# Attention in the order of a build-time list scheduler, with a third of p transposed on TensorE and q, k split before they are transposed

## The chip, the cores and the metric

The kernel runs on one core of one Trainium2 chip. The metric is the device time of one execution in microseconds; 773.15 us is the median of three runs of the kernel before (771.51 to 775.70).

## What is computed

An attention of 2 x 8 heads over 768 rows of 64 elements, masked by equality of 6-bit hash buckets, then two mixing layers on the joined heads (512 wide):

```python
q_bits = (einsum('bhsd,dk->bhsk', q, proj) > 0); k_bits = (einsum('bhsd,dk->bhsk', k, proj) > 0)
mask = bucket(q_bits)[..., :, None] == bucket(k_bits)[..., None, :]
scores = where(mask, q @ k.T / sqrt(64), -1e9)
x = softmax(scores) @ v                       # heads side by side: (2, 768, 512)
x_prev = x shifted down by one row
xk, xr = mu_k * x + (1 - mu_k) * x_prev, mu_r * x + (1 - mu_r) * x_prev
y = sigmoid(xr @ w_r) * (relu(xk @ w_k) ** 2 @ w_v)
u = y + (y.T @ U @ V).T
out = u + relu(u @ w_ch1) @ w_ch2
```

The weights come as 64-bit floats.

## The kernel before

Numbers that need more than the short format of TensorE are kept as a high and a low part, and products are made of several matmuls of parts. One core does it all, in program order on each engine.

**Attention.** Each of the 16 heads has 6 tiles of 128 rows, 96 tiles in all. Per head, q and k are loaded in natural layout (`nq`, `nk`), transposed on TensorE by threes (`prep_T`, L302) into the PSUM tile `pt`, and split there: ScalarE writes the rounded high part into one half of the partitions of `yq`, `yk` (`prep_h`, L314), VectorE the rest into the other half (`prep_l`, L319). A DMA moves the high part to a second tile `xq`, `xk` (`prep_x`, L327), `prep_z` (L334) makes the hash products, `prep_bits` (L340) their signs, and two DMAs bring these as mask rows behind x (`prep_mask`, L347). GpSimd splits v into parts (`prep_v`).

Per tile: `scores` (L369, L370; four matmuls into `ps`, one of three double banks of PSUM), `row_max` (L374), two small steps (L378, L382), `exps` on ScalarE (L388, writes `p`), `part1` (p rounded to 16 bits; L395 on ScalarE for four tiles of six, L393 on VectorE for two), `part2` on GpSimd (the rest; L124), `transp` (L404: one DMA transpose of both parts, issued from SyncE, into one of six tiles `pT`) and `weighted` (L418: 30 matmuls against v). At the end of a head come sums and division (L426 to L439); of each pair of heads `to_xT_pe` (L449) and L452 make the transposed input of the mixing layers.

**Order.** A hand-made table holds one entry for each step with an offset in tiles; for each tile number n the loop goes through it and issues the step of tile n minus offset. So `("tile", -1, "scores")` and `("tile", 6, "av")` put the product of a tile seven tiles behind its scores. `DRAIN` holds pieces of the first mixing layer (`shift_a`, `shift_b`: x mixed with the row ahead and split; `r`: nine matmuls each, eight of them) for the last tiles. `TICKS` says at which tiles the weight conversion goes one step on.

**Weights.** A job loads 64-bit words (`conv_load`, L155, three buffers `raw`), makes single precision of them on ScalarE (L167, L168), VectorE (L172, L176) and GpSimd, and splits (`conv_split`). A pipeline tick does one stage of each of the jobs under way.

**Queues.** SyncE issues the transposes, the masks of q and the weights; ScalarE issues the loads of q, k and v, the moves of y and the masks of k, between its computing.

**Behind attention** the mixing layers follow in code written out in its order: `k_half` and `halves` run k, `k_act` and v of one layer after the other, in PSUM tiles that attention leaves free. The second batch's and the channel layers are of the same kind.

## Time and profile before

| | us |
|---|---|
| median of three runs | 773.15 |
| span of the profiled execution | 780.9 |
| first exp of a tile begins | 19.23 |
| last exp ends | 306.5 |
| first matmul of the first layer's k stage | 329.2 |

| engine | busy us | share | instructions |
|---|---|---|---|
| TensorE | 700.5 | 90% | 5792 |
| VectorE | 500.2 | 64% | 866 |
| ScalarE | 390.1 | 50% | 630 |
| GpSimd | 331.4 | 42% | 252 |

The page gives the profiled execution's span, from the first to the last instruction, and no other time of it. Busy shares are means over two unlike halves; the tables of stretches separate them. [...]

### The profile page before, as it was taken

To read this page: it belongs to the slowest core of one execution; us is meant where nothing else is said; L and a number is where in the kernel's file an instruction comes from. 1 tells how busy PE (TensorE), PEld (TensorE's weight loads), DVE (VectorE), ACT (ScalarE), POOL (GpSimd) and SP (SyncE) were. 2 spreads that over 40 slices of the span, in tenths; PEclk is the share of its full clock that TensorE was granted. 3 is DMA by queue.
4 is the path that set the end of the run, shared out by engine and by line. 5 is a ranking of instruction groups with operands and counts; after the bars stand their busy time and mean duration, and the time that the engine had idled before them with its cause. 6 is when DMAs were issued, how large, how long until landed. Compare 5 with 4: busy or idle time off the path is not lost.

```text
span 780.9 us, 14599 instructions
## 1 busy us (share of the span) xinstructions
PE 700.5 (90%) x5792; PEld 614.3 (79%) x5792; DVE 500.2 (64%) x866; ACT 390.1 (50%) x630; POOL 331.4 (42%) x252
## 2 busy tenths in 40 slices
PE   4879778767798888989999999999999999999997
PEld 3668677766687776878878888888899989999996
DVE  5879997857788779589977998612578432111112
ACT  4767677655667675586546865421445221111110
POOL 1677677655676775366734754230333100000000
PEclk9889999878799999999999999999999999999999
DMA  6899999999999998123101333100334010000002
GB/s 210 140 239 210 222 207 204 220 161 167 193 206 224 182 199 128 42 87 129 48 27 55 109 109 107 54 15 14 93 124 134 1 45 37 1 1 1 0 1 81
DMA packets 180291, 86.41 MB, mean 111 GB/s; under 512 B 154432, under 2 KB 172992, under 8 KB 180224
## 3 DMA queue, kind: packets, MB, share of 16 engines
q1 hardware_dynamic: 170512, 69.36, 45.1%
q10 hardware_dynamic: 9712, 16.13, 9.4%
q8 instruction: 45, 0.74, 0.4%
q14 instruction: 22, 0.18, 0.1%
HBM read 37.10 MB, written 3.15 MB: 52 GB/s over the span
## 4 chain that ended last, share of the span: by engine, by line
PE 57%; DVE 21%; DMA 11%; issue 5%; ACT 3%; POOL 2%; SPq 1%; ACTq 1%; DVEq 0%; POOLq 0%
PE ps L605 9%; PE ps L607 8%; PE ps L606 8%; PE pt L607 7%; PE pt L605 7%; PE pt L606 7%; DMA pT<-p 7%; DVE nm L374 4%; PE pt L418 3%; DVE w L124 3%; DVE raw L172 2%; DMA xq<-zt 2%; PE ps L334 2%; ACT p L388 2%; DVE p L393 1%
## 5 line engine op out<-in xcount | busy, mean ns | idle before, releaser
L124 POOL TENSOR_TENSOR p<-p,p 128x768 f16<-128x768 f32 x96 | 159.5, 1667 | 75.3 <-ACT p L395 24.4
L676 DVE SCALAR_TENSOR_TENSOR hl<-pt,hl 128x384 fp32r<-128x384 f32 x64 | 35.7, 557 | 173.1 <-ACT hl L675 173.1
L418 PEld LDWEIGHTS <-pT 128*128 128x128 f16 x2880 | 104.4, 102 | 39.1 <-issue 31.9
L418 PE MATMUL pt<-v,pT 128*128 128x64 bf16 (+1 forms) x2880 | 115.3, 200 | 21.0 <-DVE xn L439 16.3
L675 ACT ACTIVATE hl<-pt 128x384 fp32r<-128x384 f32 x64 | 31.4, 491 | 200.2 <-PE pt L607 200.2
L124 POOL TENSOR_TENSOR cx<-cx,raw 128x512 int32<-128x512 int32 (+2 forms) x55 | 79.7, 1450 | 99.5 <-DVE cx L176 62.7
L388 ACT ACTIVATE p<-ps,nm 128x768 f32<-128x768 f32 x96 | 94.8, 989 | 54.0 <-DVE nm L382 29.5
L607 PE MATMUL ps<-w,hl 128*128 128x512 f32 x288 | 113.8, 395 | 3.5 <-DVE hl L594 3.4
L605 PE MATMUL ps<-w,hl 128*128 128x512 f32 x288 | 114.7, 398 | 2.0 <-ACT y L575 1.5
L606 PE MATMUL ps<-w,hl 128*128 128x512 f32 x288 | 113.1, 393 | 0.0
L374 DVE TENSOR_REDUCE nm<-ps 128x1 f32<-128x768 f32 x96 | 91.5, 953 | 16.3 <-PE ps L370 14.8
L369 PE MATMUL ps<-xk,xq 76*128 76x384 f32 x192 | 78.8, 411 | 14.9 <-ACT p L388 7.1
L605 PE MATMUL pt<-ut,w 128*128 128x384 f32 x256 | 86.5, 338 | 0.0
L607 PE MATMUL pt<-ut,w 128*128 128x384 f32 x256 | 86.1, 337 | 0.0
L124 DVE TENSOR_TENSOR w<-cx,w 128x512 fp32r<-128x512 f32 (+2 forms) x55 | 77.8, 1415 | 13.0 <-ACT w L208 13.0
L606 PE MATMUL pt<-ut,w 128*128 128x384 f32 x256 | 85.9, 336 | 0.0
L370 PE MATMUL ps<-yk,yq 128*128 128x384 f32 x192 | 70.4, 367 | 0.0
L607 PEld LDWEIGHTS ps<-w,hl 128*128 128x128 f32 x288 | 54.0, 188 | 19.3 <-DVE hl L594 7.9
L605 PEld LDWEIGHTS ps<-w,hl 128*128 128x128 f32 x288 | 54.1, 188 | 14.6 <-ACT y L575 2.2
L606 PEld LDWEIGHTS ps<-w,hl 128*128 128x128 f32 x288 | 54.1, 188 | 8.5
L395 ACT ACTIVATE p<-p 128x768 f16<-128x768 f32 x64 | 54.0, 844 | 9.6 <-DMA pT<-p 5.2
L369 PEld LDWEIGHTS ps<-xk,xq 76*128 76x128 f32 x192 | 40.6, 211 | 18.8 <-ACT p L388 9.9
(123 smaller groups left out, 1290.8 us busy)
## 6 DMA issues: line engine op xcount, KB each, us to landing
raw<-in_moe_w_ch_dram SPq DMA_DIRECT2D x32, 512.0 KB
raw<-in_moe_w_k_dram SPq DMA_DIRECT2D x8, 512.0 KB
raw<-in_moe_w_v_dram SPq DMA_DIRECT2D x8, 512.0 KB
nk<-in_k_dram ACTq DMA_DIRECT2D x16, 192.0 KB
xq<-yq ACTq DMA_DIRECT2D x16, 192.0 KB
xk<-yk ACTq DMA_DIRECT2D x16, 192.0 KB
v<-in_v_dram ACTq DMA_DIRECT2D x16, 192.0 KB
nq<-in_q_dram ACTq DMA_DIRECT2D x15, 192.0 KB
```

Source lines behind the costliest of these rows:

```text
L124: eng.tensor_tensor(out=out, in0=a, in1=b, op=op)
L369: nc.tensor.matmul(s_ps[:, j, 0:G], d["xq"][:, qc], d["xk"][:, c], start=True, stop=False)
L370: nc.tensor.matmul(s_ps[:, j, 0:G], d["yq"][:, qc], d["yk"][:, c], start=False, stop=True)
L374: nc.vector.tensor_reduce(out=nm[:, 0:1], in_=tl[n]["s"][:, :, 0:G], axis=AX.XY, op=ALU.max, negate=True)
L388: nc.scalar.activation(p, tl[n].pop("s")[:, :, 0:G], AF.Exp, bias=nm[:, 2:3], scale=nm[:, 1:2])
L395: nc.scalar.activation(p12[:, 0], tl[n]["p"], AF.Copy)
L418: nc.tensor.matmul(o[:, 0:d], pT[:, part, kt, :], V[a][:, kt, 0:d], start=(kt == 0 and (part, a) == (0, 1)), stop=(kt == NT - 1 and (part, ...
L605: nc.tensor.matmul(o, sh, mh, start=first, stop=False)
L606: nc.tensor.matmul(o, sh, ml, start=False, stop=False)
L607: nc.tensor.matmul(o, sl, mh, start=False, stop=last)
L675: nc.scalar.activation(hl[:, 0], self.o, AF.Relu)
L676: nc.vector.scalar_tensor_tensor(out=hl[:, 1], in0=self.o, scalar=0.0, in1=f(hl)[:, 0], op0=ALU.max, op1=ALU.subtract)
```

## The change

The order of attention is no longer a table. `Plan` collects every step as an operation with the engines that may do it and a cost for each, what it comes after, a due number and the buffers that it takes and frees; `order` goes through time and gives each free engine the ready operation with the smallest due number. Where two engines may do a step, the free one with the smaller cost gets it. The program is then issued in that order, so each engine's order is fixed when the kernel is built.

Steps that change: (1) q and k are split in natural layout, high part by ScalarE or VectorE (`prep_H`), low part by GpSimd (`prep_L`); high and low lie side by side, so two groups of three transposes (`prep_T`) give half of y each, which ScalarE copies out whole (`prep_E`); hash products and bits go by halves through the `pt` tile. (2) Tiles 1 and 4 of a head are transposed on TensorE in single precision (`flip`, six transposes into a `ps` tile), then rounded by ScalarE and subtracted by VectorE out of PSUM, with no DMA. (3) `part1` of the other tiles goes to ScalarE or GpSimd. (4) All DMAs are issued from SyncE. (5) Eight weight jobs run in attention, and the shifts of the first mixing layer are planned one by one; its eight r products come after the last tile's product and division.

```diff
+PE_TILES = (1, 4)
+JOBS_EARLY = 8
+SLOTS = {"s": 3, "t": 1, "o": 1, "n": 4, "hl_q": 1, "hl_k": 1, "y_q": 2, "y_k": 2, "x_q": 2, "x_k": 2, "zt": 2,
+         "p": 3, "p12": 4, "pT": 6, "xn": 2, "raw": 3, "cx": 4, "xh": 8, "sq": 3, "v": 2, "nm": 4}
...
+            ready.sort(key=lambda op: op.due)
+            for op in ready:
+                on = [e for e in op.on if clock[e] <= now]
+                if not on or any(free_slots[s.kind] < 1 for s in op.take):
+                    continue
+                e = min(on, key=lambda x: op.on[x])
...
+                if e == "sp":
+                    clock[e] = now + 0.1
+                    wire = max(wire, now + 1.3) + cost
+                    op.end = wire + 0.8
+                else:
+                    op.end = clock[e] = now + cost
...
+    def prep_H(i, s, e):
+        t = hd[i]["hl" + s] = ap.tile([128, NT, 2, D], F32R, name=f"hl_{s}", bufs=1)
+        copy(e, t[:, :, PART[s]], hd[i]["n" + s])
+
+    def prep_L(i, s, e):
+        t = hd[i]["hl" + s]
+        minus(e, t[:, :, 1 - PART[s]], hd[i].pop("n" + s), f(t)[:, :, PART[s]])
...
+    def flip(n):
+        f_ps = tl[n]["f"] = psum_s()
+        p = tl[n].pop("p")
+        for j in range(NG):
+            for i in range(TG):
+                c = slice(i * 128, (i + 1) * 128)
+                nc.tensor.transpose(f_ps[:, j, c], p[:, j, c], ident)
...
+        nc.scalar.activation(p1, src, AF.Copy)
...
+        minus("dve", flipped(n, 1)[0], src, p1)
...
-    def prep_h(i, s):
-    def prep_l(i, s, e):
...
+            sc = add({"pe": 0.74}, lambda e, n=n: scores(n), [*masks, *xs, *y_done], n - 1.5, take=[s_s],
+                     free=[*toks["q"], *toks["k"]], lag=0.25)
...
+            if t in PE_TILES:
+                f_s = Slot("s")
+                fl = add({"pe": 0.5}, lambda e, n=n: flip(n), [ex], n - 0.5, take=[f_s], free=[p_s], lag=0.25)
+                p1 = add({"act": 0.86}, lambda e, n=n: flip_part1(n), [fl], n - 0.5, take=[pT_s])
+                got = add({"dve": 0.98}, lambda e, n=n: flip_part2(n), [p1], n - 0.5, free=[f_s])
+            else:
+                c_s = Slot("p12")
+                p1 = add({"act": 0.87, "pool": 1.0}, lambda e, n=n: part1(n, e), [ex], n + 0.5, take=[c_s])
+                p2 = add({"pool": 1.7}, lambda e, n=n: part2(n), [p1], n + 0.5, free=[p_s])
+                got = add({"sp": 2.4}, lambda e, n=n: transp(n), [p2], n, take=[pT_s], free=[c_s])
+            avs.append(add({"pe": 0.97}, lambda e, n=n: weighted(n), [got, v2], n + 3, take=[] if avs else [o_s],
+                           free=[pT_s, v_s], lag=0.25))
...
+            r_last = add({"pe": 2.1}, lambda e, g=g, c=c: mixes[0].r(g, c), [lows[-1], r_last, sig, *tail], N + 30 + j, free=[h_s],
+                         lag=0.25)
```

On SyncE at the start of the program stood, before (`xq<-zt` is the mask of the first q; that of k was on ScalarE's queue):

```order
L239 DMA nq<-in_q_dram 128x384
L248 DMA p_raw<-in_proj_dram 64x6 x2
L459 DMA mu_k<-in_moe_mu_k_dram 128x4x1
L459 DMA mu_r<-in_moe_mu_r_dram 128x4x1
L155 DMA raw<-in_moe_w_r_dram 128x1024 x3
L347 DMA xq<-zt 12x768
```

Now, from the 14th row on, with 12 transfers of the first heads and weights ahead (three of them `raw`):

```order
L288 DMA nq<-in_q_dram 128x384
L379 DMA xk<-yk 64x768
L288 DMA nk<-in_k_dram 128x384
L379 DMA xq<-yq 64x768
L192 DMA raw<-in_moe_w_r_dram 128x1024
L288 DMA nq<-in_q_dram 128x384
L192 DMA raw<-in_moe_w_k_dram 128x4x256
L396 DMA xk<-zt 12x768
L396 DMA xq<-zt 12x768
```

The first masks stand behind the loads of two or three heads and behind five weight loads, where three stood ahead of them.

In the middle of attention stood on SyncE, before:

```order
L404 DMA_TRANSPOSE pT<-p_2308 128x12x128
L404 DMA_TRANSPOSE pT<-p_2419 128x12x128
L347 DMA xq<-zt 12x768
L404 DMA_TRANSPOSE pT<-p_2434 128x12x128
L404 DMA_TRANSPOSE pT<-p_2487 128x12x128
L404 DMA_TRANSPOSE pT<-p_2585 128x12x128
L404 DMA_TRANSPOSE pT<-p_2593 128x12x128
L404 DMA_TRANSPOSE pT<-p_2642 128x12x128
L404 DMA_TRANSPOSE pT<-p_2747 128x12x128
L347 DMA xq<-zt 12x768
L404 DMA_TRANSPOSE pT<-p_2763 128x12x128
L404 DMA_TRANSPOSE pT<-p_2816 128x12x128
```

and now, over about as many tiles:

```order
L452 DMA_TRANSPOSE pT<-p_2169 128x12x128
L452 DMA_TRANSPOSE pT<-p_2242 128x12x128
L288 DMA nk<-in_k_dram 128x384
L379 DMA xk<-yk 64x768
L379 DMA xq<-yq 64x768
L452 DMA_TRANSPOSE pT<-p_2351 128x12x128
L452 DMA_TRANSPOSE pT<-p_2363 128x12x128
L396 DMA xk<-zt 12x768
L396 DMA xq<-zt 12x768
L288 DMA nq<-in_q_dram 128x384
L452 DMA_TRANSPOSE pT<-p_2473 128x12x128
L288 DMA v_1_125<-in_v_dram 128x384
```

Six transposes of a head have become four, and the loads of q, k and v (L288), the moves of y (L379) and both masks (L396) stand between them.

On VectorE in the middle of attention stood, before (L319 is the low part of y, L393 the rounded p, L340 the hash bits; names carry their buffer numbers):

```order
L382 TENSOR_SCALAR nm_2534<-nm_2534 128x1
L393 CAST p12_2585<-p_2536 128x768
L374 TENSOR_REDUCE nm_2587<-ps_2542 128x1
L378 TENSOR_SCALAR nm_2587<-nm_2587 128x1
L319 TENSOR_TENSOR yq_2578<-pt_2538,yq_2578 64x3x128
L382 TENSOR_SCALAR nm_2587<-nm_2587 128x1
L374 TENSOR_REDUCE nm_2638<-ps_2597 128x1
L319 TENSOR_TENSOR yq_2578<-pt_2538,yq_2578 64x3x128
L378 TENSOR_SCALAR nm_2638<-nm_2638 128x1
L382 TENSOR_SCALAR nm_2638<-nm_2638 128x1
L374 TENSOR_REDUCE nm_2697<-ps_2645 128x1
L378 TENSOR_SCALAR nm_2697<-nm_2697 128x1
```

and now (L161 with `pT<-ps` is the subtraction for a tile transposed on TensorE, L349 the high part of k, L423, L427 and L431 the row maximum and the two small steps):

```order
L423 TENSOR_REDUCE nm_2941<-ps_2884 128x1
L427 TENSOR_SCALAR nm_2941<-nm_2941 128x1
L431 TENSOR_SCALAR nm_2941<-nm_2941 128x1
L161 TENSOR_TENSOR pT_2992<-ps_2950,pT_2992 128x768
L349 CAST hl_k_3009<-nk_2353 128x6x64
L423 TENSOR_REDUCE nm_3016<-ps_3002 128x1
L423 TENSOR_REDUCE nm_3032<-ps_3011 128x1
L427 TENSOR_SCALAR nm_3016<-nm_3016 128x1
L427 TENSOR_SCALAR nm_3032<-nm_3032 128x1
L431 TENSOR_SCALAR nm_3016<-nm_3016 128x1
L431 TENSOR_SCALAR nm_3032<-nm_3032 128x1
L423 TENSOR_REDUCE nm_3083<-ps_3026 128x1
```

The low parts of y and the casts of p are gone from between the row maxima, and the subtraction out of PSUM and the copies of q and k have come in; two row maxima now also stand together ahead of their small steps.

## Rows read from the trace of the kernel before

**Rows 1.** the page, parts 1 and 2: span, and DMA share in 40 equal slices.

```profile
span 780.9 us, 14599 instructions
...
DMA  6899999999999998123101333100334010000002
```

**Rows 2.** stretches; columns: us, busy PE, PEld, DVE, ACT, POOL (instructions), PEclk, DMA share, GB/s.

```profile
19.20:306.50 287.30, 230.11 (x3329) 203.23 (x3328) 233.65 (x468) 192.82 (x253) 193.22 (x136) 0.88 1.15 196
...
54.00:72.00 18.00, 16.38 (x261) 14.93 (x262) 15.77 (x33) 12.71 (x17) 13.99 (x10) 0.91 1.20 216
...
162.00:180.00 18.00, 11.90 (x147) 10.22 (x147) 10.02 (x21) 9.73 (x14) 9.69 (x7) 0.72 1.22 190
...
252.00:270.00 18.00, 14.50 (x242) 12.83 (x238) 15.12 (x33) 13.62 (x17) 13.91 (x10) 0.98 1.16 193
```

**Rows 3.** the same view of line L388 alone, the exps.

```profile
252.00:270.00 18.00, 7.56 (x8) 0.98 1.16 193
```

**Rows 4.** SyncE's queue in time (start us, us, instruction, count), then line L404's durations in ns.

```profile
93.86 16.30 SPq L404 DMA_TRANSPOSE pT<-p  x6
...
280.84 20.25 SPq L404 DMA_TRANSPOSE pT<-p  x9
...
L404 SPq DMA_TRANSPOSE pT<-p x96: 1274/2388/5505, 24.1 to 309.9; - x96
```

**Rows 5.** durations (ns, min/median/max) of other transfers' issue, by line.

```profile
L347 SPq DMA_DIRECT2D xq<-zt x16: 756/784/1553, 13.2 to 279.9; - x16
...
L327 ACTq DMA_DIRECT2D xq<-yq x16: 496/500/543, 7.9 to 265.4; - x16
...
L239 ACTq DMA_DIRECT2D v<-in_v_dram x16: 330/334/580, 19.3 to 285.4; - x16
```

**Rows 6.** the chain that ended last, in order of time: start us, us, what.

```profile
13.21 3.14 DMA xk<-zt
...
112.11 8.21 DMA pT<-p
...
130.42 4.72 DMA pT<-p
...
311.54 0.23 PE ps L606
...
319.77 0.95 PE pt L418 x30
```

**Rows 7.** VectorE by line from 19.2 to 306.5 us; the fourth: the whole run.

```profile
L374 DVE TENSOR_REDUCE nm<-ps 128x1 f32<-128x768 f32 x95 | 90.5, 953 | 16.2 <-PE ps L370 14.8
...
L393 DVE CAST p<-p 128x768 f16<-128x768 f32 x31 | 23.6, 761 | 20.2 <-ACT p L388 17.3 <-DMA pT<-p 1.9 <-ACT yq L314 0.7
...
L319 DVE TENSOR_TENSOR yk<-pt,yk 64x384 fp32r<-64x384 f32 x28 | 15.6, 556 | 0.9
...
L124 DVE TENSOR_TENSOR ut<-pt,ut 128x384 fp32r<-128x384 f32 x16 | 8.8, 552 | 10.4 <-ACT ut L208 10.4
```

**Rows 8.** ScalarE by line from 19.2 to 306.5 us.

```profile
L395 ACT ACTIVATE p<-p 128x768 f16<-128x768 f32 x64 | 54.0, 844 | 9.6 <-DMA pT<-p 5.2 <-issue 2.3 <-PE ps L370 0.2
```

**Rows 9.** GpSimd by line from 19.2 to 306.5 us.

```profile
L124 POOL TENSOR_TENSOR p<-p,p 128x768 f16<-128x768 f32 x95 | 157.8, 1667 | 74.8 <-ACT p L395 24.4 <-DVE p L393 18.2 <-DVE rl L426 17.1
...
L124 POOL TENSOR_TENSOR v<-v 128x384 f32<-128x384 f32 x32 | 27.9, 871 | 22.6 <-DMA v<-in_v_dram 20.6 <-ACT p L388 1.7 <-ACT yk L314 0.2
```

**Rows 10.** instructions in order of time: start us, us, engine, line, instruction.

```profile
60.52 0.52 PE L302 MATMUL pt<-ident,nq 128*128 128x128 f32 x3
...
60.80 0.42 PE L369 MATMUL ps<-xk,xq 76*128 76x384 f32 x1
...
19.23 0.99 ACT L388 ACTIVATE p<-ps,nm 128x768 f32<-128x768 f32 x1 [1.44 <-DVE nm L382]
...
306.52 1.65 DVE L393 CAST p<-p 128x768 f16<-128x768 f32 x1 [0.28 <-ACT p L388]
...
329.22 0.42 PE L605 MATMUL pt<-xh,w 128*128 128x384 f32 x1
```

382 lines of the change are left out of this document (229 added, 153 removed).

## The prediction

> **What bounds the kernel now.** I read the page first: the sixteen DMA engines are full in the slices up to about 300 us and nearly empty behind [rows 1]. So the run has two halves. Until 329.2 us it is attention; there the first matmul of the first mixing layer's k stage starts [rows 10]. From there to the end, 451.7 us, TensorE is busy almost without a gap and the code is the same in both kernels. What the change is worth is decided ahead of 329.2 us.
>
> I split that half at the exps, one for each of the 96 tiles. Start: 19.2 us to the first exp. Middle: 287.3 us from the first to the last, 2.99 us a tile. Drain: 22.7 us from the last exp's end at 306.5 us to 329.2 us [rows 2, 10].
>
> In the middle no computing engine is full: TensorE 230 us, VectorE 234, ScalarE 193, GpSimd 193 of 287.3, while the DMA share stands at 1.15 [rows 2]. The queue that carries it is SyncE's. Six transposes of p occupy it for 16.3 us, 2.72 us each, their median is 2.39 us, and nine with hardly a load beside them take 20.25 us, 2.25 us each [rows 4]. 96 x 2.72, 16 masks of 0.78 us and 8 weight loads, taken like the moves of y at 0.50 us [rows 4, 5], make 278 us of 287.3: the queue is the bound. The chain of waits agrees, with pieces of 8 us at a transpose [rows 6]. Where the queue lets go, eight tiles pass in 18 us [rows 3].
>
> **The change part by part.**
>
> *DMA and SyncE.* 32 of 96 transposes leave the queue, and all other transfers of attention move from ScalarE's queue into it. By issue time: 64 x 2.25 to 2.72 = 144 to 174 us, 32 masks x 0.78 = 25, 32 moves of y x 0.50 = 16, 48 loads x 0.33 = 16, 12 weight loads x 0.5 = 6 [rows 4, 5]. Together 207 to 237 us, some 10 of them ahead of the first exp, so 197 to 227 us instead of 278. It stops being the bound. A transpose that waits here for GpSimd's subtraction now holds back every load and mask behind it; the second rival prices that.
>
> *ScalarE.* It loses the issue of 47 loads (0.33), 32 moves (0.50) and 16 masks (0.79), 44 us on top of its 193 us [rows 5]. Of the rounded copies of p it keeps 23, and gains 32 of transposed tiles: nine fewer x 0.84 us [rows 8]. Splits of q and k and more shifting work put about 12 us on. Some 197 us: not the bound.
>
> *VectorE*, in the middle, from 234 us. Removed: 31 casts of p, 23.6 us, and the low parts of y, 56 x 0.555 = 31.1 us [rows 7]. Added: 32 subtractions for the transposed tiles. Before has none of this shape with its input in PSUM; the nearest are 128x384 with one input in PSUM in 0.552 us, twice that is 1.10, and the row maximum, which reads as many elements from PSUM in 0.953 us [rows 7]. I take 1.0, 32 us. Of the 32 high parts of q and k it gets 20, about 17 of them in the middle; half a cast of p is 0.38 us on the mean [rows 7], I take 0.45, 7.6 us. Copies of xT 3, weight words 5 less (more jobs are done ahead of the first exp), shifting of the first mix 4 more. 234 - 54.7 + 32 + 7.6 + 3 - 5 + 4 = 220 us; 216 to 244 between the bounds, the upper end if each high part takes the 1.65 us of the slowest cast [rows 10] (at the share taken below that is 782 us).
>
> *GpSimd*, from 193 us: 32 subtractions of p at 1.667 us fewer, -53.3; 28 low parts of q and k, like the 128x384 subtractions for v at 0.871 us [rows 9] or a little dearer, +26; other moves +2. Then 41 rounded copies of p, which the trace doesn't show on this engine. They read one operand instead of two, so from half the subtraction, 0.83 us, to all of it, 1.667. I take 1.0: 168 + 41 = 209 us, 202 to 236 between the bounds.
>
> *TensorE.* Three transposes take 0.28 us from start to start [rows 10]. Six for each of 32 tiles, 18 us, and for q and k 28 triples more in the middle, 8 us. From 230 us at a mean clock of 0.88 [rows 2], 202 at the full clock, to 228; this counts the ends of bursts, so it is an upper value. The busier stretch of 252 to 270 us had 0.98 [rows 2]; there 228 is 233 us.
>
> *So the middle* has VectorE at 220 busy us with a small pause after each of its 480 or so instructions, TensorE and GpSimd close behind. What share can VectorE reach? In two stretches where the queue hardly stopped it: 15.77 of 18 us from 54 us on, 88%, and 15.12 of 18, 84%, in the fastest [rows 2, 3]. I take 85%, since four other engines are now nearly as full: 220 / 0.85 = 259 us, 2.70 us a tile.
>
> *Start.* The masks, on which the first scores wait, are issued at 13.2 us and land 3.1 us later [rows 6]. In the new order of SyncE the second weight load ahead of them needs a raw buffer, and so the second integer addition on GpSimd. Ahead of this on GpSimd stand four low parts, four steps for v, an addition and a weight subtraction: with itself eleven operations of 0.87 us or a third more [rows 9], about 11 us with pauses. They begin when the first k is loaded and rounded, at some 8 us (an estimate; before, the whole preparation takes until 13.2). So the masks go out at 19.5 us. Two masks of 0.78, 3.1 us to land, then scores, row maximum and the two small steps: first exp at 25.5 us, 6.3 later. Lower bound none (if GpSimd is quicker than that), upper bound 10.
>
> *Drain.* After the last exp: the rounded copy 0.84 to 1.65, the subtraction 1.67, a transpose of 4.72 us when the queue is free, its product 0.95, the sums and the division about one row maximum, 1.0, three transposes 0.3, and all eight r products, which the planner holds until the attention is done: 72 matmuls x 0.23 us = 16.5 us [rows 6 to 10]. About 26.4 us for 22.7, where half of the r work lay between the last tiles. Shifts of the k part run on VectorE, ScalarE and GpSimd under those 16.5 us, two for each 4 us; without that cover they would cost 1 us each.
>
> *Behind it* one weight job more is ready; TensorE idles only some us there, so I book nothing.
>
> Sum: 25.5 + 259 + 26.4 = 310.9 for 329.2 us, -18.3 us. The profiled execution has a span of 780.9 us [rows 1] and the median of the runs is 773.15, 0.99 of it, so -18.1: **755 us**.
>
> **The rivals.** (a) *Better packing.* The list scheduler lets VectorE reach 94%: 220 / 0.94 = 234 us, -43 us, 730 us. For it: several engines are at or below 230 us. Against it: no stretch of 18 us shows it with eight tiles.
>
> (b) *The transposes' way becomes the bound; slower.* Before, the product of a tile stands on TensorE seven tiles behind its scores; now four to six, five on the mean by the order. From scores to product lie 0.7 + 0.95 + 0.4 + 0.99 + 0.84 + 1.67 = 5.6 us of work (the first and third estimated) and the transfer [rows 7 to 10]. At 4.72 us that is 10.3 us, and 2.7 us a tile leaves 14.6. At 8.21 us, as under load [rows 6], it is 13.8, with 2 to 3 us of queueing at three engines 16.5; over 5.4 tiles 3.05 us a tile, a middle of 293 us, +15.5 us, 789 us. It decides at 2.89 us a tile (277 us), once a transfer takes over about 7.5 us. For it: one queue for everything, in order. Against: a quarter of its time is free now.
>
> (c) *GpSimd's copies cost the full 1.667 us*: 236 / 0.85 = 278 us, +1 us, 774 us.
>
> (d) *TensorE at a low clock.* In 162 to 180 us its clock was 0.72 with the engine waiting for transfers [rows 2]. If new waits hold it at 0.80, 228 / 0.80 = 285 us, +7.6 us, 781 us. The Trainium skill's page TensorE: Matmul & The Clock Gate, section on PE-mode transpose, says that a transpose doesn't count as a busy TensorE for the clock; by that rule the added 26 us of transposes would favour this case. No run here shows it yet: the transposes of before are too few.
>
> (e) *Transposes were not the limit.* Then VectorE keeps the 81% that it has over the whole middle [rows 2]: 220 / 0.81 = 272 us, -5 us, 768 us. The Trainium skill's page Advanced Engine Details and Errata, section X-Bar Transpose (TRN2), says that a transposing transfer is as fast as a plain one, which speaks for this and against the change. The trace is against it: 393 KB in 2.25 us, 175 GB/s, below the 196 GB/s of the mixed middle, and the queue's own 278 us [rows 2, 4].
>
> **How the numbers follow.** Forecast (VectorE between 82 and 90%: 740 to 764 us) 50%, (a) 13%, (b) 15%, (c) 10%, (d) 7%, (e) 5%. A difference of 0.5%, 4 us, is about what a measurement of this kernel can tell from no change. Faster by more than that: the forecast and (a) wholly, a fifth of (c), over half of (e): 68%. Within it: half of (c), parts of (b), (d) and (e): 11%. Slower: the rest of (b), (c) and (d), 21%. The range from 733 to 785 leaves out half of (a) and the upper part of (b), together under 20%.
>
> **What would show it.** Right: 64 transposes on SyncE, the first exp near 25.5 us, the last ending near 284, the first k matmul near 311, and about 452 us behind it; VectorE at 85% in the middle with 1.0 us for the new subtraction; GpSimd's copies at 1.0 us. (b) shows as TensorE's products waiting for transposed p for many us in all, (c) as GpSimd over 90% busy, (d) as a mean clock under 0.85, (a) as a middle under 245 us. The forecast is wrong above all if buffers or waits, not one full engine, set the pace.

## The result, and the profile after

The changed kernel takes 785.44 us (median of four runs, 782.72 to 786.28), the kernel before 772.68 us (median of four runs): 1.0147 times as long, 95% interval 1.0108 to 1.0186. The prediction was 755 us, in a range of 733 to 785 us, and faster; the kernel became 1.5% slower.

The page of the changed kernel, parts 1 and 2, against [rows 1]: the span is the same 780.9 us, and the DMA engines, full before up to 300 us, have room.

```profile
span 780.9 us, 15090 instructions
...
PEclk9988999999999999999999999999999999999999
DMA  7599688797878767033201333100333010000002
```

Two equal spans and two unequal times: a run's time is its span and mostly 1.8 us, so the changed kernel's profiled execution (782.7 us) is one of its ordinary runs, while that of the kernel before, some 782.7 us by the same sum, is 10 us longer than the median of its ordinary runs. The experiments come back to this.

The stretch from the first to the last exp, then two parts of it (columns as in [rows 2]). TensorE is the fullest engine, and from 100 us on at its full clock.

```profile
32.60:302.30 269.70, 237.51 (x3637) 215.22 (x3636) 213.98 (x446) 181.69 (x263) 204.20 (x169) 0.97 0.81 153
...
40.00:100.00 60.00, 51.15 (x718) 46.99 (x717) 49.47 (x90) 38.32 (x56) 45.60 (x36) 0.89 0.86 167
100.00:280.00 180.00, 164.17 (x2584) 149.28 (x2583) 141.56 (x308) 123.92 (x183) 139.61 (x119) 1.00 0.83 155
```

Instructions in time at the start, answering [rows 10] (19.23 us for the first exp): the load of the first k; on TensorE the first transposes of the second head; on SyncE a weight load and the first mask behind it; on TensorE hash products of the second head and only then the scores of tile 0; the first two exps.

```profile
3.19 0.50 SPq L288 DMA_DIRECT2D nk<-in_k_dram  x1
...
18.55 0.87 PE L368 MATMUL pt<-ident,hl_k 128*128 128x128 f32 x3 [0.87 <-DVE zt L390]
...
21.34 0.38 SPq L192 DMA_DIRECT2D raw<-in_moe_w_k_dram  x1
...
21.77 0.89 SPq L396 DMA_DIRECT2D xk<-zt  x1
...
24.51 0.65 PE L385 MATMUL pt<-yk,wb_both_k 128*108 128x384 f32 x1 [0.58 <-ACT yq L347]
...
28.32 0.52 PE L418 MATMUL ps<-xk,xq 76*128 76x384 f32 x1
...
32.60 1.87 ACT L437 ACTIVATE p<-ps,nm 128x768 f32<-128x768 f32 x2 [1.51 <-DVE nm L431]
```

And at the end of attention, where the kernel before has its first k matmul at 329.22 us: the product of the last tile, the first r product behind it, and the first matmul of the k stage.

```profile
309.25 1.83 PE L488 MATMUL pt<-v,pT 128*128 128x65 bf16 x30 [2.84 <-DMA pT<-p]
...
312.71 0.78 PE L687 MATMUL ps<-w,xh 128*128 128x512 f32 x1
...
331.01 0.33 PE L687 MATMUL pt<-xh,w 128*128 128x384 f32 x1
```

By these the profiled executions split so:

| us | before | forecast | after |
|---|---|---|---|
| start, to the first exp | 19.2 | 25.5 | 32.6 |
| middle, first to last exp | 287.3 | 259 | 269.7 |
| drain, to the first k matmul | 22.7 | 26.4 | 28.7 |
| behind it | 451.7 | 451.7 | 449.9 |
| span and 1.8 | 782.7 | 764.4 | 782.7 |

### The profile page after: what moved, and what is told of

It reads as the page before. It is cut to its first block, busy times and chain, and to the rows that moved or that the text cites. A ratio compares the mean times of both kernels' runs of the same rounds, so it can differ in the third digit from the quotient of the medians.

```text
span 780.9 us, 15090 instructions
## 1 busy us (share of the span) xinstructions
PE 718.8 (92%) x6080; PEld 634.8 (81%) x6080; DVE 475.3 (61%) x830; ACT 377.8 (48%) x633; POOL 356.9 (46%) x301
## 4 chain that ended last, share of the span: by engine, by line
PE 65%; DVE 14%; DMA 6%; POOL 4%; issue 4%; ACT 4%; SPq 1%; DVEq 0%; ACTq 0%; POOLq 0%
PE ps L687 9%; PE ps L689 9%; PE ps L688 9%; PE pt L689 7%; PE pt L687 7%; PE pt L688 7%; PE pt L488 5%; DMA pT<-p 3%; DVE nm L423 2%; DVE w L161 2%; PE ps L418 2%; PE pt L368 2%; PE pt L385 2%; DVE raw L209 2%; PE ps L419 2%
## 5 line engine op out<-in xcount | busy, mean ns | idle before, releaser
L161 POOL TENSOR_TENSOR cx<-cx,raw 128x512 int32<-128x512 int32 (+2 forms) x55 | 79.8, 1451 | 89.9 <-DVE cx L213 55.5
L488 PE MATMUL pt<-v,pT 128*128 128x64 bf16 (+1 forms) x2880 | 106.8, 195 | 10.6 <-DMA pT<-p 8.0
L488 PEld LDWEIGHTS <-pT 128*128 128x128 f16 x2880 | 99.7, 98 | 20.0 <-DMA pT<-p 10.3
L161 POOL TENSOR_TENSOR p<-p,p 128x768 f16<-128x768 f32 x64 | 107.9, 1693 | 11.8 <-ACT p L347 10.5
L437 ACT ACTIVATE p<-ps,nm 128x768 f32<-128x768 f32 x96 | 92.6, 989 | 34.3 <-DVE nm L431 25.6
L423 DVE TENSOR_REDUCE nm<-ps 128x1 f32<-128x768 f32 x96 | 90.3, 951 | 21.3 <-PE ps L419 20.5
L418 PE MATMUL ps<-xk,xq 76*128 76x384 f32 x192 | 73.8, 384 | 9.9 <-ACT p L437 4.2
L161 DVE TENSOR_TENSOR w<-cx,w 128x512 fp32r<-128x512 f32 (+2 forms) x51 | 72.5, 1424 | 5.0 <-ACT w L253 3.5
L419 PE MATMUL ps<-yk,yq 128*128 128x384 f32 x192 | 67.3, 351 | 0.0
L687 PEld LDWEIGHTS ps<-w,hl 128*128 128x128 f32 x288 | 54.1, 188 | 14.2 <-ACT y L657 1.7
L349 POOL CAST p<-p 128x768 f16<-128x768 f32 x41 | 35.5, 867 | 35.1 <-ACT p L437 34.9
L687 PEld LDWEIGHTS pt<-ut,w 128*128 128x128 f32 x256 | 48.1, 188 | 2.4
```

The source lines that it names most:

```text
L161: eng.tensor_tensor(out=out, in0=a, in1=b, op=op)
L349: (nc.vector if e == "dve" else nc.gpsimd).tensor_copy(dst, src)
L418: nc.tensor.matmul(s_ps[:, j, 0:G], d["xq"][:, qc], d["xk"][:, c], start=True, stop=False)
L419: nc.tensor.matmul(s_ps[:, j, 0:G], d["yq"][:, qc], d["yk"][:, c], start=False, stop=True)
L423: nc.vector.tensor_reduce(out=nm[:, 0:1], in_=tl[n]["s"][:, :, 0:G], axis=AX.XY, op=ALU.max, negate=True)
L437: nc.scalar.activation(p, tl[n].pop("s")[:, :, 0:G], AF.Exp, bias=nm[:, 2:3], scale=nm[:, 1:2])
```

## The experiments

All tables below give the first exp, the middle and the drain of the profiled execution, and the run time: the median where the kernel was timed, else its single profiled run. "Before" was 771 to 775 us in each of these sittings.

### The kernel before once more, and without its transposition

> The kernel before, unchanged, profiled once more. The profiled execution that the prediction was worked out on has a span of 780.9 us, though its runs are 771.5 to 775.7 us, and one stretch of it (160 to 216 us) had eleven us or so more than its neighbours: 15 exps in 56 us at a granted clock of 0.78. Theory A: that execution was a long one; an ordinary one has the first exp at 19 us, the first matmul of the k stage near 320 us instead of 329.2, so a middle of about 278 us (2.89 us a tile), and 452 us behind it. Then the two kernels differ by 12 us in the middle of an ordinary execution, not by the 17.6 us that the two profiles show. Rival B: the middle of 287 us is ordinary, and the profiler makes the difference: a span of 780 us again, with the k stage at 329 us.

The profiled execution took 787.2 us, the eleven ordinary ones of the same sitting 768.5 to 780.3, median 773.7. So B of that text holds: the long middle comes with the profile. The second experiment replaces the transposing transfer of p by a plain one of the same bytes.

```diff
-        nc.sync.dma_start_transpose(
-            out=pT.rearrange("p a b c -> p (a b) c"), in_=tl[n].pop("p12").rearrange("p a g c -> p (a g c)")
+        nc.sync.dma_start(
+            out=pT.rearrange("p a b c -> p (a b c)"), in_=tl[n].pop("p12").rearrange("p a g c -> p (a g c)")
```

> The kernel before, but the transfers of p on SyncE's queue copy the same 393 KB without transposing them; the transposition is left out. Theory A (the prediction's view): the transposes of 2.25 to 2.72 us in SyncE's queue are the bound of the attention before; copied plainly the queue has room, and the middle falls from 287 to 290 us (in a profiled execution) to 250 us or less, where VectorE's 234 us and TensorE's waits set the pace. Rival B: a transposing transfer is as fast as a plain one (so the Trainium skill's page Advanced Engine Details and Errata has it, section X-Bar Transpose (TRN2)), or the queue was not the bound: the middle stays above 275 us.

> The kernel before with plain transfers of p in place of transposing ones (the transposition left out), in ordinary executions. Its profiled one took 766 us, the profiled ones of the kernel before 783 and 787 us, so 17 to 21 us; the ordinary ones of the kernel before 768 to 780 us. Theory A: the profiler's own records lengthen only executions whose DMA engines are full (share 1.15 in the middle of before, 0.65 here): ordinary executions take 763 to 768 us, like the profiled one, and the transposition was worth only 7 to 11 us to the kernel before, not the 17 to 21 us that the profiles show. Rival B: the profile lengthens every execution of this code by some 10 us: 753 to 758 us here, and the transposition is worth 17 to 21 us in ordinary executions as well.

The first took 766.05 us in its one profiled run. In the second the profiled execution took 764.6 us, the ordinary ones 763.7 to 766.4, median 764.64 (0.9889 of before, 0.9858 to 0.9921). The stretch from first to last exp of before once more, and then of the one with plain transfers:

```profile
19.70:310.10 290.40, 226.80 (x3329) 200.36 (x3328) 233.07 (x469) 193.45 (x253) 193.84 (x136) 0.89 1.15 193
```

```profile
19.40:288.30 268.90, 222.32 (x3332) 197.58 (x3331) 238.79 (x468) 192.74 (x253) 194.34 (x136) 0.90 0.65 209
```

The same number of bytes at plain order takes the DMA share from 1.15 to 0.65. The middle lies between the 250 us of A and the 275 us of B in before_plain, so neither holds as told; in before_plain2 A holds. In profiled executions the transposition is worth 18 to 22 us, in ordinary ones 774.29 - 764.64 = 9.7 us. Where the DMA engines have room, profiled and ordinary runs agree. So the kernel before, in an ordinary run, has a middle of about 277 us (an estimate: 772.7 less 1.8, 451.7, 22.7 and 19.2; no trace of an ordinary run is kept). Without any transposition VectorE stands at 89% of 268.9 us; whether it is the limit there, no run tests. The queue was full, as the prediction said, but what could be won at it in that order was 10 us.

### No tile on TensorE

```diff
-PE_TILES = (1, 4)
+PE_TILES = ()
```

> The changed kernel with PE_TILES empty: no tile of p is transposed on TensorE, all 96 go through SyncE's queue, planned by the same list scheduler. TensorE loses 28 us of its 237.5 busy us in the middle, VectorE 31, ScalarE 26 less the rounded copies that it takes again, GpSimd gains 53. Theory A: the transposes through the queue were the limit (2.25 to 2.7 us each), so the middle goes from 269.7 us to 280 to 290 us, the whole to 793 to 806 us. Rival B: the queue was not the limit, but TensorE is (88% busy in the middle of the changed kernel): the middle gets shorter or stays, the whole is 770 to 786 us. Rival C: GpSimd becomes the bound with 96 subtractions of 1.69 us and its share of copies (204 + 53 us of busy time): ScalarE takes the copies and the middle is 285 us or more with GpSimd over 90% busy.

800.99 us, 1.0368 of before (1.033 to 1.0407), as A has it; middle 292.3 us, 2.3 over A's range:

```profile
32.90:325.20 292.30, 236.34 (x3411) 205.38 (x3412) 200.22 (x425) 189.14 (x271) 239.16 (x182) 0.91 1.01 181
```

The DMA share is 1.01, and GpSimd is at 82%, not over 90% as C had it. The transposition on TensorE does what it is for: 22.6 us of middle by the two profiles, 15.6 us by the run times. The profiled execution took 805.4 us, the others 799.9 to 801.7, so some 5 us of the 22.6 may come with the profile. What costs is the rest: the other parts of the change, with all tiles in the queue, are slower than the kernel before by 27 us.

### The start and the drain

In this run the weight loads stand behind the first exp in the plan and the second head's transposes behind the scores of tile 0.

```diff
-        last = ld = add({"sp": 2.1}, lambda e, j=j: conv_load(j), due=due - 10, take=[raw_s])
+        last = ld = add({"sp": 2.1}, lambda e, j=j: conv_load(j), [ex0], due=due - 10, take=[raw_s])
...
-                tr = add({"pe": 0.27}, lambda e, i=i, s=s, g=g: prep_T(i, s, g), [lo], due - 8 + g, take=[t_s],
+                tr = add({"pe": 0.27}, lambda e, i=i, s=s, g=g: prep_T(i, s, g), [lo, first[0] if i == 1 else None], due - 8 + g, take=[t_s],
```

> The changed kernel with two edits to its planner: the loads of the weight jobs wait for the first exp, and the transposes of the second head's q and k wait for the scores of tile 0. In the changed kernel the first exp starts at 32.6 us (19.2 before, 25.5 forecast). Theory A: two things in series make it late, the masks of head 0 behind a weight load on SyncE that waits until 21.3 us for GpSimd's addition, and on TensorE two rows of the second head (transposes 18.55 to 23.9 us, hash products 24.5 to 28.3 us) ahead of the scores of tile 0. With both moved, the masks are issued near 17 us, the first exp starts at 21 to 23 us, and the whole kernel gains 8 to 11 us: 773 to 777 us. Rival B: the start is not on the path of the whole, since the work that is moved (weight jobs, the second head) holds up the first tiles instead: first exp at 21 to 23 us, but the first k matmul moves by less than 4 us: 780 to 785 us.

782.55 us (1.0124 of before, 1.0082 to 1.0165), 2.9 us less than the changed kernel. The masks go out at 18.2 us and the first exp comes at 27.1 us instead of 32.6, so the two together cost 5.5 us, though 4 to 6 us more remain than A had; but the middle is 277.6 us, 7.9 more. B is nearer: the first k matmul comes only 0.4 us earlier. In the middle VectorE has 226 us here for 214 and GpSimd 215 for 204, so work that was moved comes back there.

What remains at the start lies in part in the change itself. The first transposes of the kernel before, then those of start_both and its first mask:

```profile
4.07 0.87 PE L302 MATMUL pt<-ident,nk 128*128 128x128 f32 x3 [4.07 <-DMA nk<-in_k_dram]
```

```profile
7.45 0.90 PE L368 MATMUL pt<-ident,hl_k 128*128 128x128 f32 x3 [7.45 <-POOL hl_k L161]
...
18.21 0.89 SPq L396 DMA_DIRECT2D xk<-zt  x1
```

Before, TensorE waited for the load only; now k is rounded and subtracted first, and the transposes begin 3.4 us later. The masks go out 5.0 us later (13.2 us before), with no weight load ahead of them.

In the next run the r products wait for the last exp and the last transposition only.

```diff
-    tail = [*avs, nr]
+    tail = [ex, fl]
```

> The changed kernel with one edit to its planner: the eight r products wait for the last exp and the last transposition on TensorE, not for the last tile's products and the division of the last head. In the changed kernel all 72 matmuls of r run from 312.7 to 331.0 us, behind everything, and TensorE waits 2.9 us for the last transfer and 1.2 us for the division ahead of them. Theory A: with this the first r products lie in those waits and between the last tiles' products, and the first nine no longer run at 1.2 GHz after an idle stretch: the end of the attention moves up by 4 to 8 us, the whole to 777 to 781 us. Rival B: the last transfer and the sums end the attention in any case and the r products in front of the last tiles only delay these: within 2 us of the changed kernel, 783 to 787 us.

778.01 us (1.0064 of before, 1.0038 to 1.009), 7.4 us less than the changed kernel, as A has it. By the two traces the first k matmul comes 4.1 us earlier; the rest is that the changed kernel's profiled run lies 2.7 us under its median and this one's 0.6 over. TensorE in time in this run: 18 r matmuls lie ahead of the last tile's product, at a granted clock of 1.00 from 308.7 to 312.9 us. The changed kernel starts its first eight about 0.43 us apart, at a mean clock of 0.60 (first line), and the later ones 0.23.

```profile
312.70:316.70 4.00, 4.00 (x15) 3.19 (x14) 0.00 (x0) 0.64 (x2) 0.00 (x0) 0.60 0.00 0
```

```profile
308.70 0.48 PE L687 MATMUL ps<-w,xh 128*128 128x512 f32 x1
...
312.90 1.11 PE L488 MATMUL pt<-v,pT 128*128 128x65 bf16 x30
...
326.94 0.33 PE L687 MATMUL pt<-xh,w 128*128 128x384 f32 x1
```

The drain is 22.7 us, as before the change; the middle is 271.8 us.

### The weight work, and all edits together

On top of drain, weight job j is loaded behind the exp of tile 10(j - 2).

```diff
-        last = ld = add({"sp": 2.1}, lambda e, j=j: conv_load(j), due=due - 10, take=[raw_s])
+        last = ld = add({"sp": 2.1}, lambda e, j=j: conv_load(j), [exs[10 * (j - 2)] if j > 2 else None], due=due - 10, take=[raw_s])
```

> The kernel of the run drain, with one edit more: the load of weight job j (from the fourth on) stands in the plan behind the exp of tile 10(j - 2), so that the eight weight jobs lie along the whole attention. In the changed kernel all eight are worked off before 75 us, and the exps come at 20 in 60 us from 40 to 100 us (3.0 us a tile), but at 71 in 180 us from 100 to 280 us (2.54 us a tile). Theory A: the early crowd of weight work on VectorE, GpSimd and the transfers is what makes 40 to 100 us slow; spread, its work lies under TensorE, which is the fullest engine behind 100 us (92% busy, VectorE 77%). Then 40 to 100 us holds 22 or 23 exps and the rest keeps 2.55 to 2.62 us a tile: the whole 4 to 8 us under the run drain, 770 to 774 us. Rival B: the first 100 us are slow because the pipeline fills and the clock of TensorE is 0.84 there; the weight work only moves and costs as much later: 776 to 781 us.

772.4 us (0.9991 of before, 0.9955 to 1.0027): the time of A, but not its way. The text's 71 exps in 180 us count those across an edge twice; the busy time of the exps, 64.1 us at 0.99, gives 2.78 us a tile from 100 to 280 us for the changed kernel and 3.5 from 40 to 100 us. In spread (20.2 and 58.75 us of exps) it is 2.9 from 40 to 100 us and 3.0 behind: the slow part became quicker and the quick part slower, and the middle is 269.0 us against 271.8 in drain. The first exp comes 2.7 us earlier, at 29.7. Half of the gain is the start.

Then best1 puts the edits together and loads the first k and q ahead of all else:

```diff
     ctx.enter_context(tc.manual_schedule())
+    load_head(0, "k")
+    load_head(0, "q")
...
-        last = ld = add({"sp": 2.1}, lambda e, j=j: conv_load(j), due=due - 10, take=[raw_s])
+        last = ld = add({"sp": 2.1}, lambda e, j=j: conv_load(j), [exs[min(9 * j, 90)]], due=due - 10, take=[raw_s])
```

> The changed kernel with all that the runs so far point to: the r products behind the last exp (as in drain), weight job j behind the exp of tile 9j, the second head's transposes behind the scores of tile 0 (as in start_both), and the loads of the first k and q at the head of SyncE's queue, ahead of the projection and the shift vectors. In start_both these loads are issued at 3.19 us (0.74 in the kernel before), and the first exp starts at 27.1 us. Theory A: the losses lie in different places and add up: first exp at 24 to 25 us, 95 tiles at 2.65 us, drain at 22.8 us, 449.8 us behind: 749 + 1.8 us at the best, with the slower first tiles 752 to 768 us, faster than the kernel before. Rival B: what is saved at the start is given back, as in start_both, where the middle grew by 7.9 us while the first exp came 5.5 us earlier: 772 to 780 us.

769.82 us (0.9949 of before, 0.9912 to 0.9986): first exp 27.9 us, middle 269.3, drain 23.0. It is half a percent faster than the kernel before and 15.6 us faster than the changed one, if 2 us short of A: the gains at both ends stay (4.7 and 5.7 us by the traces), the first exp is 3 us later than told, the middle doesn't move.

The early load wins nothing. It is issued at 0.74 us instead of 3.19. But VectorE rounds this k behind its small steps on the projection, whose load now comes later: at 6.98 us, where start_both has 5.97. The first exp comes 0.8 us after that of start_both.

```profile
0.74 0.40 SPq L288 DMA_DIRECT2D nk<-in_k_dram  x1
...
6.98 0.35 DVE L350 CAST hl_k<-nk 128x384 fp32r<-128x384 f32 x1
```

### What sets the middle

Four cuts, each alone, take work from one engine or from the queue; the order of the changed kernel's plan stays.

```diff
-            for part, a in ((0, 1), (0, 0), (0, 2), (1, 0), (1, 1)):
+            for part, a in ((0, 1), (0, 0), (1, 0), (1, 1)):
```

> The changed kernel, but one of the five products of each p block with v is left out (the high half of p with the third part of v): 6 of 30 matmuls of 0.195 us for each tile, 1.2 us of 5.8 by their own durations, about 0.42 us a tile of TensorE's busy time (198 us for 92 tiles now). Theory A: TensorE sets the pace behind 100 us, where it is 92% busy and a tile takes 2.54 us: the tiles from 100 us on take 2.15 to 2.25 us, the middle falls from 269.7 us to 235 to 245 us, the whole to 748 to 760 us. Rival B: no engine sets it, but the way from scores to product and the buffers on it: the middle falls by 10 us or less, 773 to 783 us. Rival C: VectorE is next (2.2 us a tile of busy time): the middle lands between, near 255 us.

The diff of the second is that of before with plain transfers, in `transp`.

> The changed kernel, but the 64 transfers of p on SyncE's queue copy their 393 KB without transposing them; the transposition is left out. In the kernel before, the same step took the middle from 287 to 290 us down to 270 us, with VectorE 89% busy. Theory A: in the changed kernel no more than the way of single tiles hangs on the transfers (TensorE waits 18 us for them in all): the middle goes from 269.7 us to 260 to 267 us. Rival B: they still set the pace through the buffers that they hold (p12, pT): the middle goes below 255 us. Rival C: no effect at all, 268 us or more, since the order of the plan and the other engines set it.

```diff
-        minus("pool", p12[:, 1], tl[n].pop("p"), p12[:, 0])
+        copy("pool", p12[:, 1], tl[n].pop("p"))
```

> The changed kernel, but GpSimd's 64 subtractions p - high(p) are replaced by rounded copies of p (the low part is left out): 64 x (1.69 - 0.87) = 52 us less of its 204 busy us in the middle. Theory A: GpSimd, fed late by ScalarE (it waits 35 us for exps) and 76% busy, is on the way of every tile that goes through the queue: the middle falls from 269.7 us by 10 to 25 us. Rival B: GpSimd has slack like the others and the middle stays within 6 us.

```diff
-        nc.vector.tensor_reduce(out=nm[:, 0:1], in_=tl[n]["s"][:, :, 0:G], axis=AX.XY, op=ALU.max, negate=True)
+        nc.vector.tensor_reduce(out=nm[:, 0:1], in_=tl[n]["s"][:, 0, 0:G], axis=AX.X, op=ALU.max, negate=True)
```

> The changed kernel, but the row maximum is taken over the first 384 of 768 scores only (half of that work is left out): 96 x about 0.45 = 43 us less of VectorE's 214 busy us in the middle, and 0.45 us less between scores and exp. Theory A: VectorE with its maximum ahead of every exp sets the pace (ScalarE waits 33 us for it): the middle falls from 269.7 us by 20 to 40 us. Rival B: VectorE has slack (79% busy) and the middle falls by 8 us or less.

And all four in one kernel:

> The changed kernel with all four cuts at once: one of five products of p with v left out, the transfers of p not transposing, GpSimd's subtractions replaced by rounded copies, the row maximum over half of the scores. Alone they moved the middle by -1.1, -4.2, -4.4 and -4.5 us from 269.7 us; simply added that is 255.5 us. Theory A: several engines and the queue are near their limits together, so each cut alone only uncovers the next; cut together, the middle falls to 225 to 248 us. Rival B: the order of the plan, the ways between engines and the buffers set the pace, whatever the engines' work: the middle stays at 254 to 265 us.

| run | cut | middle, us | run, us |
|---|---|---|---|
| changed kernel | none | 269.7 | 785.44 (profiled 782.72) |
| av4 | TensorE's products | 268.6 | 781.43 |
| after_plain | the transposition | 265.5 | 776.17 |
| pool_half | GpSimd | 265.3 | 777.03 |
| dve_half | VectorE | 265.2 | 778.97 |
| all4 | all of these | 246.5 | 753.47 |

By the numbers A holds in after_plain and B in the other three. Each is one profiled execution, and two profiles of before with plain transfers differ by 1.2 us in the middle, so the 1.1 us of av4 is no effect and the other three are alike. Neither GpSimd nor VectorE sets the pace alone. The stretch of the middle in pool_half, then in dve_half: 55 us of GpSimd's work gone, 33 us of VectorE's, and TensorE's busy time hardly moves.

```profile
32.40:297.70 265.30, 238.68 (x3635) 217.45 (x3636) 203.83 (x446) 181.75 (x263) 149.52 (x169) 0.96 0.85 156
```

```profile
32.90:298.10 265.20, 237.28 (x3623) 216.53 (x3623) 180.60 (x446) 180.99 (x263) 203.30 (x169) 0.97 0.82 156
```

For TensorE, av4 settles less than its text expects. A tile's 30 product matmuls take 0.94 us from their start to the next instruction's, 24 of them 0.74 (in the changed kernel, then in av4):

```profile
201.09 0.82 PE L463 MATMUL ps<-ident,p 128*128 128x128 f32 x6
201.74 1.10 PE L488 MATMUL pt<-v,pT 128*128 128x65 bf16 x30
202.68 0.52 PE L368 MATMUL pt<-ident,hl_k 128*128 128x128 f32 x3
```

```profile
204.44 0.91 PE L488 MATMUL pt<-v,pT 128*128 128x65 bf16 x24
205.18 0.42 PE L418 MATMUL ps<-xk,xq 76*128 76x384 f32 x1
```

So the cut is 0.2 us a tile and not 0.42: the text's 198 us add the busy times of two groups of matmuls that overlap. And the granted clock was lower in this run, so that TensorE's busy time in the middle fell by 5.7 us only (237.5 to 231.8). A run that takes so little can't show that TensorE doesn't set the pace. The middle of av4, and its products and scores from 100 to 280 us (columns: count, busy us, mean ns, idle before); the changed kernel has 1.00 there in place of 0.95, and 194 and 373 ns.

```profile
32.90:301.50 268.60, 231.79 (x3091) 207.16 (x3091) 214.65 (x445) 181.25 (x263) 203.18 (x169) 0.93 0.82 153
...
100.00:280.00 180.00, 160.82 (x2217) 144.69 (x2218) 141.90 (x308) 123.41 (x183) 139.32 (x120) 0.95 0.83 154
...
L488 PE MATMUL pt<-v,pT 128*128 128x65 bf16 x792 | 62.1, 198 | 4.6 <-DMA pT<-p 3.1 <-DVE nm L431 0.9 <-POOL p L161 0.3
...
L418 PE MATMUL ps<-xk,xq 76*128 76x384 f32 x129 | 49.9, 387 | 3.2 <-DMA xq<-zt 1.6 <-ACT p L437 1.1 <-DMA xk<-zt 0.4
```

Together the cuts give 23.2 us, more than the 14.2 us of their sum. That is A of all4, near the end of its range, and fits several limits close together, where a cut at one uncovers the next. In all4:

```profile
32.00:278.50 246.50, 223.05 (x3085) 200.12 (x3084) 168.92 (x446) 179.78 (x263) 149.48 (x169) 0.97 0.53 169
```

VectorE and GpSimd are at 69% and 61% there, TensorE at 90% still. That it takes 246.5 us and not less is TensorE, or the ways between the engines in an order that was planned for more work; the runs don't tell these two apart.

The last edit to the middle of best1 that is not a cut: the plan counts longer transfers, and p12 has five buffers.

```diff
-                    op.end = wire + 0.8
+                    op.end = wire + 2.8
...
-         "p": 3, "p12": 4, "pT": 6, "xn": 2, "raw": 3, "cx": 4, "xh": 8, "sq": 3, "v": 2, "nm": 4}
+         "p": 3, "p12": 5, "pT": 6, "xn": 2, "raw": 3, "cx": 4, "xh": 8, "sq": 3, "v": 2, "nm": 4}
```

> The run best1, with two edits more: the plan counts 2 us more from the end of a transposing transfer to its product (it counted 4.5 us from issue to product for an idle queue; the trace shows 4.3 to 5.5), so products stand further behind their scores, and a fifth buffer for the rounded pairs of p, as the kernel before has. Theory A: waits of TensorE for single late transfers hold the middle of best1 at 269.3 us: it falls by 5 to 12 us, the whole to 758 to 765 us. Rival B: these waits are short and their place is taken by others: 767 to 773 us, as best1. Rival C: longer ways hold more buffers, and the plan runs out of them: 774 us or more.

776.53 us (1.0029 of before, 0.9995 to 1.0062), middle 275.6 us: the time of C. TensorE's matmuls hardly wait for transposed p any longer (3.6 us in best1), but 15.4 us for exps, where it was 8.4.

### How many tiles on TensorE

Best1 with other tiles in `PE_TILES`; in the second and third run every second head has them.

> The run best1 with one tile of a head (tile 3) transposed on TensorE instead of two: 16 tiles move back to SyncE's queue. TensorE loses 14 us of its 239 us in the middle (89% busy there), the queue gains 16 transposes of 2.3 us. Theory A: TensorE is nearest to its limit and the queue still has room (80 x 2.3 + 55 = 239 us of 269): the middle falls by 3 to 10 us, the whole to 760 to 767 us. Rival B: the queue is as near: 768 to 773 us, no difference. Rival C: it goes over (without any tile on TensorE the middle was 292 us): 774 to 785 us.

> The run best1 with two tiles on TensorE in every second head and one (tile 3) in the others: 8 tiles move back to the queue. Theory A, as in best_1f: TensorE gives 7 us, the middle falls by 2 to 6 us, the whole to 763 to 768 us. Rival B: no difference, 768 to 773 us. Rival C: slower, 774 us or more.

> The run best1 with tiles 0, 2 and 4 of every second head transposed on TensorE, tiles 1 and 4 of the others: 8 tiles more than best1, TensorE 7 us more, GpSimd about 14 to 20 us less, the queue 8 transposes of 2.3 us less. Theory A: the queue and GpSimd are the nearer limit: the middle falls by 2 to 4 us, the whole to 765 to 768 us. Rival B: TensorE is (239 + 7 = 246 us at 90% gives 273 us): the middle grows by 2 to 5 us, the whole to 771 to 776 us.

> The run best1 with tiles 0, 2 and 4 of every head transposed on TensorE: 16 tiles more than best1, TensorE 14 us more, VectorE 15 us more, the queue 16 transposes less. Theory A: the queue and GpSimd are the nearer limit even so: the middle falls by 4 to 8 us, the whole to 761 to 766 us. Rival B: TensorE is (239 + 14 = 253 us at 90% gives 281 us): the middle grows by 6 to 12 us, the whole to 776 to 782 us.

The middle of best1, of one tile and of three:

```profile
27.90:297.20 269.30, 239.32 (x3604) 215.86 (x3605) 221.37 (x463) 184.38 (x271) 219.34 (x183) 0.97 0.86 168
```

```profile
28.30:307.60 279.30, 234.85 (x3484) 209.45 (x3485) 220.41 (x448) 189.62 (x277) 234.18 (x187) 0.96 0.94 181
```

```profile
27.70:304.60 276.90, 247.81 (x3736) 225.89 (x3737) 231.82 (x471) 200.05 (x294) 181.07 (x154) 0.99 0.69 141
```

| tiles of six | TensorE | VectorE | GpSimd | DMA share | middle, us | run, us |
|---|---|---|---|---|---|---|
| 1 | 234.8 | 220.4 | 234.2 | 0.94 | 279.3 | 786.58 |
| 1.5 | 235.7 | 227.9 | 226.3 | 0.93 | 273.1 | 775.37 |
| 2 (best1) | 239.3 | 221.4 | 219.3 | 0.86 | 269.3 | 769.82 |
| 2.5 | 244.1 | 227.5 | 195.1 | 0.78 | 275.3 | 779.88 |
| 3 | 247.8 | 231.8 | 181.1 | 0.69 | 276.9 | 778.9 |

One tile and one and a half: C, the former 1.6 us over its range. Two and a half and three: B, with 6.0 and 7.6 us of middle; the former is 3.9 us over its range of run times. Two is the best count that was tried. The shares suggest the queue and GpSimd as the nearer limit below it and TensorE above it, which is about 89% busy with two tiles or more here. That is argued, not shown: VectorE's work grows too, and each count has other tiles and a new order.

## Why the prediction was wrong

The error is 785.4 - 755.0 = 30.4 us. By the steps of the prediction it is made of 9.4 us of base, 7.1 of start, 10.7 of middle, 2.3 of drain, -1.8 behind it, and 2.7 by which the changed kernel's median lies over its profiled run. Against an ordinary run of the kernel before the change costs 13.4 us at the start and 6.0 in the drain, and wins 7.6 in the middle (by the estimate of 277 us) and 1.8 behind.

**The base: wrong.** The prediction took its saving from a middle of 287.3 us and then multiplied it by 0.99. It had both numbers, 780.9 us of span and runs of 771.5 to 775.7, and read the difference as a scale. It is 10 us of one stretch, the one that the change relieves, as far as profiles tell: the two of before and the two with plain transfers agree within 0.5 us in all other stretches. By the estimate ordinary runs have 277 us there; the changed kernel's profile is not lengthened. Of the 17.6 us that the two profiles show as saved in the middle, ordinary runs then get 7 to 8. The two profiled executions of before (some 782.7 and 787.2 us) lie 10 and 14 us over the medians of its ordinary runs, of which the longest in any sitting was 782.6; noflip, with a share of 1.01, has 805.4 profiled and 799.9 to 801.7 otherwise; kernels with a share up to 0.94 (best_1f) show nothing of the kind. That the records of the profile share the DMA engines with the kernel would explain it, but is only argued.

**The queue as bound: right, but worth less.** The 64 transposes and the room in the queue came as told, noflip shows the effect of `flip` (15.6 us of run time), and after_plain gives only 4.2 us more. But in the kernel before the next limit stood some 8 us away (a middle of 268.9 us without the transposition, 277 with it), as rival (e) feared for other reasons.

**The middle: the terms nearly right, the step to one full engine wrong.** The durations held but for one: the changed kernel's subtraction out of PSUM took 0.955 us (1.0 taken), GpSimd's copies 0.87 (1.0), the high parts of q and k on VectorE about 0.8 (0.45). VectorE has 214 us (220), GpSimd 204 (209); ScalarE 182 is 15 under the forecast. TensorE has 237.5 us at a clock of 0.97; the forecast's 228 at the full clock are 235 there, by its own way of converting. In the middle, by line, on VectorE, GpSimd and TensorE:

```profile
L161 DVE TENSOR_TENSOR pT<-ps,pT 128x768 f16<-128x768 f32 x31 | 29.6, 955 | 13.3 <-ACT pT L471 12.8
L349 DVE CAST hl_k<-nk 128x384 fp32r<-128x384 f32 x9 | 7.5, 833 | 0.6 <-PE pt L368 0.6
```

```profile
L349 POOL CAST p<-p 128x768 f16<-128x768 f32 x40 | 34.6, 869 | 33.3 <-ACT p L437 33.1
```

```profile
L463 PE MATMUL ps<-ident,p 128*128 128x128 f32 x192 | 28.1, 285 | 3.2 <-ACT p L437 3.1
L368 PE MATMUL pt<-ident,hl_q 128*128 128x128 f32 x84 | 14.6, 284 | 4.1 <-ACT yk L347 3.4 <-DVE xT L349 0.7
L368 PE MATMUL pt<-ident,hl_k 128*128 128x128 f32 x83 | 14.6, 285 | 3.5 <-ACT yq L347 1.7 <-POOL xh L161 1.1 <-DVE zt L390 0.7
```

A tile's six transposes have 0.88 us of busy time, but their end lies under the next burst: from start to the next start they take 0.65 us (201.09 to 201.74 us above), where 0.56 was taken. The fault is the step 220 / 0.85 = 259 us, which let VectorE set the pace. It reached 79%, and cutting 33 us of its work gave 4.5 us. GpSimd, at 76%, gave 4.4 us for 55. TensorE, at 88%, may be what the middle waits for most, or it is the ways and buffers, as the last sentence of the prediction had feared; this stays open.

The Trainium skill, on the page Perfetto Trace Analysis, section Identifying the Most-Contended Engine, warns that matmul busy time is no good measure of how near TensorE is to its limit, because matmuls are pipelined, and would judge by the utilization in arithmetic (MFU) and the busy share of weight loads. Here that share and the busy share of matmuls move together: 80 and 88% in the middle of the changed kernel, 77 and 86% in av4, 81 and 90% in all4. No run shows which of them tells the limit better.

**The start: a second cause was missed.** The first was seen: a weight load ahead of the masks waits for GpSimd's addition; masks at 21.8 us instead of 19.5. But on TensorE too the second head's transposes and hash products, each half waiting for the one `pt` tile, stand ahead of the scores of tile 0, to 28.3 us: the part of TensorE's order from 18.5 us on was not read. Nor was it priced that the split now comes ahead of the transposes, which begin 3.4 us later (start_both). That the first k is loaded at 3.19 us behind four small transfers (0.74 us before) costs little: VectorE, busy with the projection until then, waits 0.16 us for it, and best1, which loads it at 0.74, wins nothing by it. With (b)'s prices for scores, row maximum and small steps the listed terms also add up to 26.2 us, not 25.5. The bounds, nothing to 10 us later than before, didn't hold the 13.4.

**The drain: nearly right.** The r products behind everything are what costs. The last product took 1.83 us instead of 0.95 and the first eight r matmuls 0.43 us each instead of 0.23, at the lower clock behind waits of 2.8 and 1.1 us; that was not in the sum.

**The rivals.** (a), (c) and (d) didn't occur: no better packing, copies of 0.87 us, a mean clock of 0.97. (b) is a small part of its price: TensorE waits for transposed p, but without the transposition the middle is 4.2 us shorter, not the 34 us between (b)'s 293 and the forecast's 259. That (b)'s 789 us lies near the measured time is chance; its sum also takes 5.4 tiles from scores to product, where its text counts five. The Trainium skill's page TensorE: Matmul & The Clock Gate, section on PE-mode transpose, says that a transpose doesn't count as a busy TensorE in the same way, which made (d) likelier. No low clock came with the added transposes: with 48 tiles transposed on TensorE (best_3f) the middle's clock is 0.99, with none (noflip) 0.91. But TensorE is also idle more in noflip, 81% busy for 89%, so the rule itself is not tested. The Trainium skill's page Advanced Engine Details and Errata, section X-Bar Transpose (TRN2), says that transposing transfers are as fast as plain ones. The runs are against it: a DMA share of 1.15 against 0.65 for the same bytes, and 9.7 us of run time.

## What to carry to other kernels

Set a profiled execution against the ordinary runs of the same kernel before using it as a base, and find the stretch in which the difference lies: it may be the one that a change relieves. When several engines are 75 to 90% busy, don't divide one engine's work by a share; cut each engine's work in turn, then all at once, see by its busy time how much a cut took, and expect single cuts to give little. Where a planner sets the order, read what stands ahead of the first piece on every engine and behind the last one: here best1 won 10.4 us at both ends and 0.4 us in the middle.

## What the runs showed of the hardware

Profiled executions of a kernel whose DMA share is over 1 took 5 to 14 us longer than the median of ordinary ones (before, noflip); at 0.65 to 0.94 they were within 3.3 us, above or below. A transposing transfer costs the DMA engines far more than a plain one of the same 393 KB (a share of 1.15 against 0.65 in the middle), though leaving all 96 of them plain won only 9.7 us of 774. And in the one run with a fifth of the products taken away from TensorE its granted clock was 0.95 instead of 1.00 between 100 and 280 us, and its scores took 387 ns instead of 373; best1, with all of them in another order, has 0.96 there, so that the cut lowered the clock is likely but not shown.
